# Moving the exponent multiplication of 64-bit weights from ScalarE to POOL

## The chip, the cores and the metric

The kernel runs on one core of a Trainium2 chip. A core has five engines that take instructions from queues of their own and wait for each other by semaphores: TensorE (PE, with its weight loads PEld), VectorE (DVE), ScalarE (ACT), GpSimd (POOL) and SyncE (SP), which here issues all transfers. The metric is the device time of one execution in microseconds (us).

## The reference

Four batches, eight heads, 768 positions, 64 dimensions a head. Attention is banded: a position sees the 127 before it, itself, and the first four ("sinks"). The attention's output is the input of a gated two-layer network.

```python
scores = q @ k.T / sqrt(64)
keep = (key < n_sink) | ((0 <= rel) & (rel < window))     # n_sink 4, window 128
a = softmax(where(keep, scores, -1e9));  x = a @ v        # x: (4, 768, 512)
h = maximum(x @ w_in, 0)                                  # w_in: 512 x 1024
conv = sum(conv_w[k] * shifted(h, k - 1) for k in 0..2)   # along the positions
out = (h * sigmoid(conv)) @ w_out                         # w_out: 1024 x 512
```

q, k and v are 32-bit floats. The three weights w_in, conv_w and w_out arrive as 64-bit floats.

## The kernel before

The work has three parts that run interleaved. Attention goes over pairs of heads: `scores` (lines 488 to 522) makes TensorE multiply, VectorE add the mask and find the smallest value (line 514), ScalarE take the exponential (line 517), VectorE sum and invert (519, 520), and POOL scale the result (line 522). `transp` then turns the tiles on TensorE (line 538 or 552), ScalarE copies them out (540 or 554), and `pv` multiplies by v. The network goes over units of 128 hidden features by 256 positions (`unit`, line 162): twelve multiplications into `ph` (line 183), the gate on ScalarE and VectorE (190 to 198), POOL's high and low part of the gated product (lines 200 and 201), and six multiplications into `po` (line 210). The main loop of `banded` (line 644) lays pieces of the network between the steps of attention.

The third part prepares the weights. `weights` (line 131) lists 17 pieces: eight of w_in (wi), eight of w_out (wo), each 128x512, and the taps of conv_w, 24x128. `need` (line 154) prepares them one by one, about one for each step of attention from the third on, and `fetch` (line 149) asks for the next transfers on SP's queue. A raw piece holds pairs of 32-bit words, and `narrow` (line 103) makes one 32-bit float of each pair: a multiplication of the high word, taken as a 32-bit float, by 2 to the power -112 (line 111), and three steps on VectorE which shift that by three bits and put in the top bits of the low word and the sign (lines 112 to 114). `split` (line 117) then has ScalarE write the rounded high part (line 121) and POOL the remainder (line 122).

The temporaries `w` and `low` of `narrow` come from three buffers (tag `st`, line 109), the raw pieces from three others (tag `nat`). A buffer is given out again when its last reader is done, so the multiplication of one piece can wait for the subtraction of an earlier one, and a load on SP for the second VectorE step of an earlier one.

The kernel is built with `schedule_with_timeline_sim=True` (line 821): a planner fixes the order of the instructions on each engine at build time, from the order of the program and from its own costs. On the chip each engine takes its instructions in that fixed order. All pieces of the trace here come from the branch `banded`.

Of the kernel before, what the change touches and what calls it, by code (L numbers as in the profile page):

```python
# [14 lines left out]
ALU = mybir.AluOpType  # L15
# [22 lines left out]
def f(ap):  # L38
    return ap.bitcast(F32)
# [21 lines left out]
class Moe:  # L61
# [41 lines left out]
    def narrow(self, raw):  # L103


        if raw.dtype == F32:
            return raw
        nc, (rows, n) = self.c.nc, raw.shape[0:2]
        w, low = (self.temp("st", 512, 3)[0:rows, 0:n] for i in range(2))
        lo, hi, wi, li = raw[:, :, 0], raw[:, :, 1], w.bitcast(I32), low.bitcast(I32)  # L110
        nc.scalar.mul(low, f(hi), 2.0 ** -112)
        nc.vector.tensor_scalar(wi, li, 3, None, ALU.logical_shift_left)
        nc.vector.scalar_tensor_tensor(out=wi, in0=lo, scalar=29, in1=wi, op0=ALU.logical_shift_right, op1=ALU.bitwise_or)  # L113
        nc.vector.scalar_tensor_tensor(out=wi, in0=li, scalar=-0x80000000, in1=wi, op0=ALU.bitwise_and, op1=ALU.bitwise_or)  # L114
        return w
# [709 lines left out]
```

## Time and profile before

| What | Value |
|---|---|
| Time, median of 3 runs | 495.17 us (494.23 to 495.84) |
| Span of the profiled execution | 492.3 us |
| The profiled execution's own time beside its span | not stated by the page; the runs' median is 2.9 us above the span |
| Instructions | 10616 |
| Busy: TensorE, ScalarE, VectorE, POOL | 460.4, 349.0, 341.1, 308.6 us |

The page's first part gives each engine's busy time and its share of the span. Its second part cuts the span into 40 equal slices of 12.3 us; each digit is the busy share of a slice in tenths, and PEclk is TensorE's granted clock in the same way. A line number such as L111 stands for line 111 of the kernel. In the tables by stretch each engine's busy time is followed by its number of instructions in brackets. In lists by time the columns are start, length, engine, line, operation, what is written from what, shape and count, and in square brackets the idle time before it with the instruction that ended it.

### The profile page before, as it was taken

What the parts mean: (1) busy time and instruction counts of PE and PEld (TensorE: products, weight loads), DVE (VectorE), ACT (ScalarE), POOL (GpSimd) and SP (SyncE); (2) the same over time, 40 slices, a digit from 0 to 9 for tenths busy, and PEclk for the clock granted to TensorE, in tenths of its full rate; (3) what the DMA queues carried; (4) which work ended last, traced back from release to release, by engine and by line L of the source; (5) the groups of instructions that cost most, each with busy time, mean ns of one, the idle gap of its engine ahead of it and who ended that gap; (6) DMA issues with size and microseconds to landing.
All of it is one profiled execution on the core that took longest, in us unless ns stands there. A gap on an engine that the chain in (4) does not pass through costs nothing.

```text
span 492.3 us, 10616 instructions
## 1 busy us (share of the span) xinstructions
PE 460.4 (94%) x3253; PEld 396.5 (81%) x3253; DVE 341.1 (69%) x1164; ACT 349.0 (71%) x1090; POOL 308.6 (63%) x582
## 2 busy tenths in 40 slices
PE   2878889899999999999999999999999999999994
PEld 1656678687887888888888888888889888999982
DVE  4678899847587787886677767776675664555551
ACT  3888897877797887886777777786776664535542
POOL 3467677845958787794867677684764554444341
PEclk9989899999999999999999999999999999999999
DMA  5877673427332423334042322224021100101001
GB/s 148 212 198 213 180 192 89 100 60 190 75 82 56 121 65 71 81 100 108 17 109 67 87 79 62 66 62 99 23 54 34 45 0 1 45 1 45 14 30 51
DMA packets 87306, 41.02 MB, mean 83 GB/s; under 512 B 80160, under 2 KB 80184, under 8 KB 87240
## 3 DMA queue, kind: packets, MB, share of 16 engines
q1 hardware_dynamic: 87240, 40.25, 31.3%
q8 instruction: 28, 0.46, 0.4%
q14 instruction: 38, 0.31, 0.2%
HBM read 27.60 MB, written 6.29 MB: 69 GB/s over the span
## 4 chain that ended last, share of the span: by engine, by line
PE 71%; DVE 7%; ACT 7%; POOL 6%; DMA 3%; issue 3%; SPq 1%; POOLq 0%; DVEq 0%; ACTq 0%
PE ph L183 25%; PE po L210 24%; PE px L591 6%; PE sc L337 3%; PE sc L338 3%; PE pts L552 3%; PE tq L271 2%; PE px L594 2%; ACT roomL L517 1%; PE tk L289 1%; DVE stm L114 1%; POOL pe L522 1%; DVE t L196 1%; DVE stm L113 1%; DMA wi_1r<-in_moe_w_in_dram 1%
## 5 line engine op out<-in xcount | busy, mean ns | idle before, releaser
L210 PE MATMUL po<-woH,g 128*128 128x512 f32 x384 | 141.6, 407 | 4.2 <-POOL g L200 4.2
L183 PE MATMUL ph<-xH,wiH 128*128 128x258 f32 (+1 forms) x384 | 113.2, 295 | 0.4 <-ACT xH L345 0.4
L183 PE MATMUL ph<-xL,wiH 128*128 128x258 f32 (+1 forms) x384 | 109.6, 286 | 0.0
L183 PE MATMUL ph<-xH,wiL 128*128 128x258 f32 (+1 forms) x384 | 109.5, 285 | 0.0
L200 POOL TENSOR_SCALAR g<-t 128x256 fp32r<-128x256 f32 x96 | 42.1, 439 | 63.6 <-DVE t L198 49.3
L210 PEld LDWEIGHTS po<-woH,g 128*128 128x128 f32 x384 | 68.8, 189 | 15.2 <-POOL g L200 5.5
L195 DVE SCALAR_TENSOR_TENSOR t<-hb,cw,t 128x256 f32<-128x256 f32 x96 | 55.1, 574 | 36.1 <-ACT t L194 35.4
L201 POOL TENSOR_TENSOR g<-t,g 128x256 fp32r<-128x256 f32 x96 | 75.9, 790 | 6.3
L522 POOL TENSOR_SCALAR pe<-pe,sm 128x132 f32<-128x132 f32 (+1 forms) x144 | 59.5, 425 | 30.7 <-DVE sm L520 20.6
L183 PEld LDWEIGHTS ph<-xH,wiH 128*128 128x128 f32 x384 | 73.1, 190 | 5.7 <-issue 1.6
L210 PE MATMUL po<-woL,g 128*128 128x512 f32 x192 | 75.8, 395 | 0.0
L183 PEld LDWEIGHTS ph<-xH,wiL 128*128 128x128 f32 x384 | 73.1, 190 | 2.2
L183 PEld LDWEIGHTS ph<-xL,wiH 128*128 128x128 f32 x384 | 72.9, 190 | 1.0 <-DVE xL L346 0.2
L517 ACT ACTIVATE pe<-pe,sm 128x132 f32<-128x132 f32 (+1 forms) x144 | 58.0, 405 | 14.1 <-DVE sm L514 13.5
L197 ACT ACTIVATE t<-t 128x256 f32<-128x256 f32 x96 | 40.3, 420 | 31.2 <-DVE t L196 30.5
L198 DVE SCALAR_TENSOR_TENSOR t<-t,hb 128x256 f32<-128x256 f32 x96 | 47.4, 494 | 17.7 <-ACT t L197 17.0
L196 DVE SCALAR_TENSOR_TENSOR t<-hb,cw,t 128x256 f32<-128x256 f32 x96 | 54.8, 570 | 4.4
L190 ACT ACTIVATE hb<-ph 128x258 f32<-128x258 f32 (+1 forms) x96 | 37.0, 386 | 29.2 <-PE ph L183 28.7
L194 ACT ACTIVATE t<-hb,cw 128x256 f32<-128x256 f32 x96 | 49.2, 513 | 7.1 <-POOL g L201 3.2
L556 POOL TENSOR_SCALAR_AFFINE_SELECT pT<-pT 128x256 f32<-128x256 f32 x60 | 29.4, 490 | 30.0 <-ACT pT L554 29.5
L513 DVE COPY_PREDICATED sc<-before,sc 128x128 f32<-128x128 int32 x120 | 34.0, 291 | 18.0 <-PE sc L338 17.1
L514 DVE CUSTOM_DVE_ANT_0 pe<-sc,m 128x132 f32<-128x132 f32 (+1 forms) x144 | 40.1, 289 | 7.7 <-PE sc L338 6.2
(148 smaller groups left out, 1005.9 us busy)
## 6 DMA issues: line engine op xcount, KB each, us to landing
raw<-in_q_dram SPq DMA_DIRECT2D x64, 96.0 KB
raw<-in_k_dram SPq DMA_DIRECT2D x64, 96.0 KB
out_dram<-stm SPq DMA_DIRECT2D x24, 256.0 KB
kk<-kk SPq DMA_DIRECT2D x24, 198.0 KB
vraw<-in_v_dram SPq DMA_DIRECT2D x24, 192.0 KB
wi_0r<-in_moe_w_in_dram SPq DMA_DIRECT2D x2, 512.0 KB
wi_1r<-in_moe_w_in_dram SPq DMA_DIRECT2D x2, 512.0 KB
wi_2r<-in_moe_w_in_dram SPq DMA_DIRECT2D x2, 512.0 KB
```

Of the source, the lines that this page charges most:

```text
L183: nc.tensor.matmul(u.h[:, 0:W], w[:, cc, ff * P:(ff + 1) * P], x[:, cc, t0:t1], start=(i == 0), stop=(i == len(prods) - 1))
L194: nc.scalar.mul(a, prev, cw[:, 0, ff:ff + 1])
L195: nc.vector.scalar_tensor_tensor(out=e, in0=this, scalar=cw[:, 1, ff:ff + 1], in1=a, op0=ALU.mult, op1=ALU.add)
L196: nc.vector.scalar_tensor_tensor(out=a, in0=nxt, scalar=cw[:, 2, ff:ff + 1], in1=e, op0=ALU.mult, op1=ALU.add)
L197: nc.scalar.activation(e, a, AF.Tanh)
L198: nc.vector.scalar_tensor_tensor(out=a, in0=e, scalar=1.0, in1=this, op0=ALU.add, op1=ALU.mult)
L200: nc.gpsimd.tensor_scalar(u.g[:, 0], a, 1.0, 1.0, ALU.mult, ALU.mult)
L201: nc.gpsimd.tensor_tensor(out=u.g[:, 1], in0=a, in1=f(u.g[:, 0]), op=ALU.subtract)
L210: nc.tensor.matmul(po[:, 0:c.DM], u.g[:, a, tt * P:(tt + 1) * P], w[:, ff, :], start=(ff == 0 and i == 0), stop=(ff == NFF - 1 and i == 2))
L514: nc.vector.tensor_tensor_reduce(out=pe[:, j, cols], in0=pc[:, P - at:SW][:, cols], in1=mk, op0=ALU.add, op1=ALU.min, scale=1.0, scalar=3. ...
L517: nc.scalar.activation(pe[:, j, cols], pe[:, j, cols], AF.Exp, bias=sm[:, j:j + 1], scale=-1.0, accum_out=sm[:, 2 + 2 * j:3 + 2 * j])
L522: nc.gpsimd.tensor_scalar(pe[:, j, cols], pe[:, j, cols], sm[:, 8 + j:9 + j], 1.0, ALU.mult, ALU.mult)
```

## The change

One line of `narrow` is replaced. The same product is computed by POOL; the second multiplication, by 1.0, leaves it as it is. The 17 instructions read every second 32-bit word of the raw piece and write a contiguous tile, as before.

```diff
55.00:62.00 7.00, 1.36 (x2) 0.81 0.56 149
62.00:70.00 8.00, 0.70 (x1) 1.00 0.70 200
70.00:75.00 5.00, 0.69 (x1) 1.00 0.67 187
75.00:90.00 15.00, 1.38 (x2) 1.00 0.28 63
 -108,7 +108,7 55.00:62.00 7.00, 1.36 (x2) 0.81 0.56 149
62.00:70.00 8.00, 0.70 (x1) 1.00 0.70 200
70.00:75.00 5.00, 0.69 (x1) 1.00 0.67 187
75.00:90.00 15.00, 1.38 (x2) 1.00 0.28 63

         nc, (rows, n) = self.c.nc, raw.shape[0:2]
         w, low = (self.temp("st", 512, 3)[0:rows, 0:n] for i in range(2))
         lo, hi, wi, li = raw[:, :, 0], raw[:, :, 1], w.bitcast(I32), low.bitcast(I32)
-        nc.scalar.mul(low, f(hi), 2.0 ** -112)
+        nc.gpsimd.tensor_scalar(low, f(hi), 2.0 ** -112, 1.0, ALU.mult, ALU.mult)
         nc.vector.tensor_scalar(wi, li, 3, None, ALU.logical_shift_left)
         nc.vector.scalar_tensor_tensor(out=wi, in0=lo, scalar=29, in1=wi, op0=ALU.logical_shift_right, op1=ALU.bitwise_or)
         nc.vector.scalar_tensor_tensor(out=wi, in0=li, scalar=-0x80000000, in1=wi, op0=ALU.bitwise_and, op1=ALU.bitwise_or)
```

## Rows read from the trace of the kernel before

**Rows 1.** The page's first part: busy time and share of each engine.

```profile
PE 460.4 (94%) x3253; PEld 396.5 (81%) x3253; DVE 341.1 (69%) x1164; ACT 349.0 (71%) x1090; POOL 308.6 (63%) x582
```

**Rows 2.** The table by stretch, four stretches of the span in us; after the length come PE, PEld, DVE, ACT and POOL busy, the granted clock, the share of the transfer engines and GB/s.

```profile
10.00:55.00 45.00, 35.16 (x212) 26.35 (x213) 34.66 (x123) 39.18 (x120) 25.25 (x37) 0.95 0.76 212
55.00:90.00 35.00, 32.55 (x247) 28.54 (x246) 31.85 (x78) 30.47 (x82) 27.41 (x30) 0.96 0.49 129
90.00:100.00 10.00, 7.88 (x41) 5.41 (x40) 8.25 (x31) 8.18 (x27) 8.28 (x14) 1.00 0.48 112
100.00:492.00 392.00, 383.34 (x2753) 335.02 (x2751) 262.17 (x918) 268.97 (x858) 243.63 (x479) 1.00 0.25 63
```

**Rows 3.** The same table for the instructions of line 111 alone; the second number is ScalarE's busy time.

```profile
10.00:55.00 45.00, 7.09 (x11) 0.95 0.76 212
55.00:62.00 7.00, 1.36 (x2) 0.81 0.56 149
62.00:70.00 8.00, 0.70 (x1) 1.00 0.70 200
70.00:75.00 5.00, 0.69 (x1) 1.00 0.67 187
75.00:90.00 15.00, 1.38 (x2) 1.00 0.28 63
```

**Rows 4.** What TensorE waited for, from 0 to 60 us and, the last row, from 60 to 130 us: total, times, longest.

```profile
PE trq L313 <- DMA raw<-in_q_dram: 3.2, 2, 2.9
PE sc L334 <- DVE sm L514: 3.1, 4, 1.5
PE tk L545 <- ACT sk L544: 1.9, 1, 1.9
...
PE po L210 <- POOL g L200: 3.0, 2, 2.0
```

**Rows 5.** The pieces of line 111 on the chain of work that ended last: start, length, what.

```profile
18.14 0.68 ACT stm L111
...
35.25 0.56 ACT stm L111
...
37.28 0.57 ACT stm L111
...
46.51 0.71 ACT stm L111
...
50.08 0.59 ACT stm L111
...
79.01 0.61 ACT stm L111
```

**Rows 6.** The table by stretch again (columns as in rows 2), for three stretches.

```profile
35.00:40.00 5.00, 4.91 (x40) 3.41 (x39) 4.79 (x24) 5.00 (x20) 2.53 (x5) 1.00 0.45 134
55.00:70.00 15.00, 15.00 (x123) 13.12 (x121) 13.84 (x42) 13.70 (x39) 11.01 (x14) 0.91 0.63 176
75.00:80.00 5.00, 4.60 (x41) 3.87 (x41) 4.88 (x9) 3.74 (x9) 2.55 (x2) 1.00 0.18 41
```

**Rows 7.** Waits around the multiplication: one instruction of POOL and one of ScalarE in order of time with the idle time before them, VectorE's wait for the multiplication between 10 and 90 us, and SP's wait before weight loads.

```profile
21.64 0.94 POOL L522 TENSOR_SCALAR roomH<-roomH,sm 128x260 f32<-128x260 f32 x2 [3.10 <-DVE sm L519]
...
46.51 0.71 ACT L111 ACTIVATE stm<-wo3r 128x512 f32<-128x512 f32 x1 [0.91 <-POOL woL L122]
...
DVE stm L112 <- ACT stm L111: 2.2, 3, 1.5
...
SPq L100 <- DVE stm L113: 16.4, 9, 3.3
```

**Rows 8.** POOL's nearest operations: two rows of a line's summary (shortest, median and longest in ns, first and last start) and two pairs in order of time.

```profile
L200 POOL TENSOR_SCALAR g<-t x96: 397/404/842, 71.2 to 484.0; 128x256 fp32r<-128x256 f32 x96
...
L122 POOL TENSOR_TENSOR wiL<-stm,wiH x8: 1262/1280/1718, 14.0 to 69.8; 128x512 fp32r<-128x512 f32 x8
...
22.55 0.72 POOL L522 TENSOR_SCALAR roomL<-roomL,sm 128x128 f32<-128x128 f32 x2
23.78 0.94 POOL L522 TENSOR_SCALAR roomL<-roomL,sm 128x260 f32<-128x260 f32 x2 [0.51 <-ACT wiH L121]
```

**Rows 9.** POOL, VectorE and TensorE in order of time around 70 us, POOL's next gap, and the third VectorE step of an earlier piece.

```profile
66.60 3.21 POOL L522 TENSOR_SCALAR roomL<-roomL,sm 128x260 f32<-128x260 f32 x4 [1.01 <-DVE sm L520]
69.78 1.43 POOL L122 TENSOR_TENSOR wiL<-stm,wiH 128x512 fp32r<-128x512 f32 x1
70.01 1.75 DVE L114 SCALAR_TENSOR_TENSOR stm<-stm,stm 128x512 int32<-128x512 int32 x1
72.07 0.50 PE L210 MATMUL po<-woH,g 128*128 128x512 f32 x1 [2.05 <-POOL g L200]
...
80.19 0.57 POOL L200 TENSOR_SCALAR g<-t 128x256 fp32r<-128x256 f32 x1 [2.39 <-DVE t L198]
...
38.72 0.68 DVE L114 SCALAR_TENSOR_TENSOR stm<-stm,stm 128x512 int32<-128x512 int32 x1
```

**Rows 10.** POOL and VectorE side by side: two scalings and the second VectorE step beside them, and the third VectorE step between 10 and 90 us as a group (busy us, mean ns).

```profile
29.92 1.37 POOL L522 TENSOR_SCALAR roomH<-roomH,sm 128x128 f32<-128x128 f32 x2 [1.19 <-DVE sm L520]
30.31 0.74 DVE L113 SCALAR_TENSOR_TENSOR stm<-wi_3r,stm 128x512 int32<-128x512 int32 x1
...
L114 DVE SCALAR_TENSOR_TENSOR stm<-stm,stm 128x512 int32<-128x512 int32 x16 | 16.5, 1029 | 0.1
```

## The prediction

> **What bounds the kernel now.** I read the page's busy shares first. TensorE is busy for 460.4 of 492.3 us, the next engine for 349.0 [rows 1], so the kernel is TensorE's over most of its length, and a change on other engines can only pay where TensorE stands idle. The table by stretch says where that is [rows 2]. From 100 us on TensorE is busy for 383.34 of 392.00 us. Between 10 and 55 us it is busy for 35.16 of 45.00, so idle for 9.8; between 55 and 90 us for 32.55 of 35.00, idle for 2.5; between 90 and 100 us idle for 2.1. All 17 instructions of the change lie between 10 and 90 us, eleven in the first of these stretches (7.09 us) and six in the second: two before 62 us, one in front of 70, one in front of 75 and two behind it, 4.13 us in all [rows 3]. What the change can win is therefore a part of about 12 us of idle time, and what it can lose is new idle time in the same place: every microsecond that the first 90 us get shorter or longer moves the TensorE-bound rest by as much.
>
> Next I read what TensorE waited for there [rows 4]. The input transfers' 3.2 us are not touched. Left are waits on VectorE's masked copies of the scores (3.1 us), on ScalarE (the longest 1.9 us) and, after 60 us, on POOL's high part of the gated product (3.0 us in two waits). So in this stage three engines take turns as the one that is late, and two of them have little room: between 10 and 55 us ScalarE is busy for 39.18 us of 45 (87%), VectorE for 34.66, POOL for 25.25; between 55 and 90 us VectorE leads with 31.85 of 35 (91%), ScalarE has 30.47, POOL 27.41 [rows 2].
>
> **What goes.** ScalarE loses 7.09 + 4.13 = 11.2 us, by the rows of the line itself. It falls to 32.1 of 45 us (71%) and 26.3 of 35 us (75%). Six of the 17 stand on the chain of waits, with 0.68, 0.56, 0.57, 0.71, 0.59 and 0.61 us, 3.7 us in all [rows 5]; that is the bound of what taking them off the chain gives, since the other eleven had something later beside them. I go through the six. The one at 18.14 us lies in a stretch where ScalarE's work follows without a gap until TensorE has waited 1.9 us for it, while POOL sat idle for 3.1 us [rows 7]: I count 0.6 gained. Those at 35.25 and 37.28 lie where TensorE is busy for 4.91 of 5.00 us [rows 6]; the cover there is TensorE's own work, and I count them at nothing (1.1 if that cover is gone). At 46.51 ScalarE stood 0.91 us waiting for the buffer that POOL's subtraction held before it could begin [rows 7]; on POOL that wait is gone, since the reader that holds the buffer is the instruction before it on the same queue. But the score copies that ScalarE does next come from VectorE, which was itself in a long third step of the unpacking, so of the 1.6 us (0.91 and 0.71) I count 0.6. At 50.08 VectorE waited for the result, and it will wait for POOL's in the same way: 0.2. The one at 79.01 lies where TensorE is 92% busy: nothing. The sum is -1.4 us, between 0 and -3.7 by the chain; with the 0.91 us wait in front of one of them, -4.6.
>
> **What comes.** POOL gets 16 operations of 128x512 and one of 24x128. The trace has no POOL operation with one input and 512 columns, and none that reads every second word, as this one does. The nearest row is the same form on 256 columns, 404 ns in the median and never under 397 [rows 8]. Two pairs of the softmax scaling give the price of a column: two of 260 columns take 0.94 us and two of 128 take 0.72, so 0.11 us for 132 columns, 0.83 ns each; 256 more columns make 404 + 213 = 617 ns. From below the bound is the 0.40 us of half the size; from above it is the two-input subtraction on 512 columns, 1.28 us in the median. I take 0.65 us, near the extrapolated row. That is 16 x 0.65 + 0.3 = 10.7 us (6.7 to 20.8): in the first stretch 6.8 us and in the second 3.9 us, which brings POOL to 32.1 of 45 (71%) and 31.3 of 35 (89%).
>
> Where this lies beside other work it is free, and in the first stretch it mostly does. Between 66.6 and 72 us it isn't: POOL runs four scalings, a weight subtraction and the first high part of a gated product without a gap, and TensorE stands 2.05 us for the last of them [rows 9]. The one multiplication between 62 and 70 us can fall in front of it: +0.65. Of those behind 75 us one or both fall into 2.39 us in which POOL waited for VectorE [rows 9], and the two between 55 and 62 lie where TensorE is never idle (15.00 of 15.00) [rows 6]; if either cover went, they would cost 0.65 each.
>
> Then VectorE. Its third unpacking step takes 0.68 us where nothing disturbs it, but 1.75 us beside a subtraction of POOL that had begun 0.2 us earlier and lasted 1.43 [rows 9]. It can also be POOL that pays: two scalings of 128 columns that take 0.72 us elsewhere took 1.37 beside the second step, which itself lost nearly nothing (0.74) [rows 10]. So the engines hold one another up, and a new POOL operation can hold VectorE up by as long as it lasts, or by nothing. I take half of an operation, 0.3 us, for the two multiplications between 62 and 75 us, where VectorE is 91% busy and TensorE isn't always full, and count one of the two as landing on a free VectorE: +0.3. The bounds are 0 and 6 x 0.65 = 3.9 for the whole second stretch.
>
> The Trainium skill, SBUF — State Buffer on-chip working memory, Summary: rules for kernel authors, says that VectorE and GpSimd don't share bandwidth there but exclude each other for whole instructions, when VectorE runs in a two-port mode or has two SBUF inputs and GpSimd reads SBUF. By that rule every multiplication that meets a second or third unpacking step, which read two tiles, holds it up to its own end or is held up itself; that is the case which rival 2 prices from rows. The trace agrees so far as its two cases in rows 9 and 10 go: in each, one engine lost about the remainder of the other's instruction.
>
> **What waits anew.** VectorE's shift by three waits for the multiplication; behind it on VectorE are score copies, and TensorE waits for those. Today that wait costs VectorE 2.2 us in three times [rows 7]. SP's queue is behind it too: a weight load waits until the second unpacking step has read an earlier buffer (16.4 us, nine times) [rows 7], and the q, k and v loads are queued behind it. If POOL is later than ScalarE, these are later; as POOL has 20 us without work in the first stretch, I cost it at nothing, and 2.2 us more if it is as late again as ScalarE was. Everything after 90 us is unchanged in kind.
>
> **Sum.** -1.4 + 0.65 + 0.3 = -0.45 us. It is made against the profiled execution, whose span is 492.3 us; the page gives no other time for it, and the median of the runs, 495.17, lies 2.9 us above that span, so I take the difference over to the median: 494.7 us. By its bounds: -4.6 + 0 at the best end, and 0 + 3.9 + 0.65 at the worst, less the covers.
>
> **Rivals.** (1) The relief of ScalarE counts in full: at 87% busy it is the most loaded engine of the first stretch, and a shorter queue there brings every exponential and every copy forward, also those beside which the chain now runs. For it speak the ScalarE waits in rows 4 and POOL's idle time; against it VectorE, at 77% and 91%, which doesn't lose work. It would give -3.7 on the chain and +0.65: 492.1 us. (2) Slower: POOL and VectorE become the bound from 55 us on. Place: the six multiplications after 55 us, in POOL's and VectorE's fullest stretch; price: 0.65 us each, 3.9 us, against at most 0.9 us that the first stretch has won by then; it decides as soon as POOL finds less than about 4 us idle in these 35 us, that is if an operation takes 1.28 us rather than 0.65 (27.41 + 7.7 = 35.1 of 35). That gives +3.0: 498.2 us. For it speak [rows 9, 10], against it the full TensorE between 55 and 70 us [rows 6]. (3) The move does what it says but the order matters more: the program's order on each engine is written by a planner at build time, and a changed cost there can bring other instructions forward. Nothing in the trace gives this a sign; within 2 us of today by the size of TensorE's single longest waits [rows 4], either way.
>
> **How the numbers follow.** The forecast gets 0.42, its own range 492.9 to 496.6. Rival 1 gets 0.28, rival 2 0.25, rival 3 0.05. A measurement of this kernel can tell about 0.3% from no change, 1.5 us. Of the forecast's chance 0.07 lies below 493.7, 0.03 above 496.7; rival 1 gives 0.26 of faster, rival 2 0.25 of slower, rival 3 splits. Together: faster 0.35, same 0.34, slower 0.31. The range from 490.8 to 499.0 takes in most of both rivals.
>
> **What would show it.** In the changed profile line 111 must stand on POOL, 17 times, about 0.62 to 0.75 us each; over 1.0 us would speak for rival 2. ScalarE's busy time must be lower by about 11 us between 10 and 90 us. The idle time of TensorE between 10 and 55 us should fall from 9.8 to about 8.5 us, that between 55 and 100 us should rise from 4.6 to about 5.5. If VectorE's third unpacking step, in the mean 1.03 us, grows to 1.3 or more, the price of the mutual hold-up was set too low. The forecast is wrong if TensorE's idle time before 100 us changes by more than 2 us in sum, or if that after 100 us changes by over 1 us, which no step here accounts for.

## The result and the profile after

The changed kernel takes 501.07 us in the median (499.56 to 501.66, four runs), beside 495.21 us (494.23 to 495.84, four runs) for the kernel before: ratio 1.0116, 95% interval 1.0095 to 1.0138. It is slower, by 5.7 us on 495.2, and lies outside the range of 490.8 to 499.0 us. (In the code cut of the change further up, four lines of [rows 3] stand twice ahead of the code; they are figures of the profile. The change is the one line with the minus and the one with the plus.)

One reading aid first. The changed kernel's profiled execution took 499.56 us with a span of 497.8, and in the runs below an execution's own time is likewise 1.7 to 1.9 us above its span. For the profile of before, whose own time wasn't stated, the span of 492.3 us so means about 494.1 us, the quick end of its runs. Two profiles can therefore stand some 2 us further apart, or closer, than two medians. Differences in us below are the ratio to before taken on 495.2 us, unless a trace is named.

Busy shares of the changed kernel, which answer to [rows 1]:

```profile
PE 462.9 (93%) x3253; PEld 395.3 (79%) x3253; DVE 349.6 (70%) x1164; ACT 340.6 (68%) x1073; POOL 321.2 (65%) x599
```

Its table by stretch, the columns as in [rows 2], and then the same table for the instructions of line 111 alone, which answers to [rows 3]:

```profile
10.00:55.00 45.00, 34.27 (x223) 25.53 (x224) 36.00 (x121) 34.49 (x111) 32.29 (x47) 1.00 0.76 205
55.00:90.00 35.00, 29.12 (x207) 24.01 (x206) 33.48 (x77) 24.08 (x65) 31.22 (x35) 0.90 0.47 131
90.00:100.00 10.00, 9.46 (x56) 7.89 (x54) 6.70 (x21) 7.73 (x24) 8.73 (x13) 1.00 0.35 76
...
10.00:95.00 85.00, 12.06 (x17) 0.96 0.62 168
```

The move did what it says: between 10 and 90 us ScalarE is busy for 58.6 us instead of 69.7, and POOL makes the 17 multiplications in 12.06 us, 0.71 in the mean (0.74 for the 16 of 128x512). But TensorE's idle time rose in both long stretches, from 9.84 to 10.73 us (45.00 less 34.27) and from 2.45 to 5.88; only between 90 and 100 us did it fall, from 2.12 to 0.54. In sum it is 17.2 us instead of 14.4. VectorE, which lost and gained no instruction, is busy for longer: 36.00 against 34.66 and 33.48 against 31.85 [rows 2].

The three unpacking steps of VectorE show where. The table for 10 to 95 us, for lines 112, 113 and 114 alone; before first:

```profile
10.00:95.00 85.00, 8.99 (x17) 0.96 0.63 171
10.00:95.00 85.00, 12.39 (x17) 0.96 0.63 171
10.00:95.00 85.00, 16.73 (x17) 0.96 0.63 171
```

And after:

```profile
10.00:95.00 85.00, 12.60 (x17) 0.96 0.62 168
10.00:95.00 85.00, 14.77 (x17) 0.96 0.62 168
10.00:95.00 85.00, 14.55 (x17) 0.96 0.62 168
```

The same 17 pieces, the same instructions, and 41.9 us instead of 38.1. The first step, with a single input, grew by 40%. That the third fell isn't the move's doing: with ScalarE multiplying in the changed kernel's order (e2 below) it takes 13.98 us, and the three together 35.8, so that in its own order the move lengthened them by 6.1 us. One piece of the timeline after shows how (start, length, engine, line):

```profile
33.22 0.29 POOL L111 TENSOR_SCALAR stm<-tapsr 24x128 f32<-24x128 f32 x1
33.50 0.93 POOL L522 TENSOR_SCALAR roomH<-roomH,sm 128x260 f32<-128x260 f32 x2
33.55 2.19 DVE L112 TENSOR_SCALAR stm<-stm 24x128 int32<-24x128 int32 x1 [0.80 <-POOL stm L111]
34.40 1.25 POOL L122 TENSOR_TENSOR wiL<-stm,wiH 128x512 fp32r<-128x512 f32 x1
...
36.42 0.24 PE L128 MATMUL cwt<-ident,stm 24*128 24x24 f32 x1 [2.68 <-DVE stm L114]
```

VectorE is released by POOL's multiplication, but POOL, in order, goes straight on to two scalings and a subtraction. The small step begins 0.05 us after the scalings and ends at 35.74, just after the subtraction does at 35.65: 2.19 us for 24x128. TensorE waits 2.68 us for the result. That wait is new beside those in [rows 4].

### The profile page after: what moved, and what is told of

Its sections match the earlier page's. It is cut to its first block, busy times and chain, and to the rows that moved or that the text cites. A ratio compares the mean times of both kernels' runs of the same rounds, so it can differ in the third digit from the quotient of the medians.

```text
span 497.8 us, 10601 instructions
## 1 busy us (share of the span) xinstructions
PE 462.9 (93%) x3253; PEld 395.3 (79%) x3253; DVE 349.6 (70%) x1164; ACT 340.6 (68%) x1073; POOL 321.2 (65%) x599
## 4 chain that ended last, share of the span: by engine, by line
PE 75%; DVE 8%; POOL 4%; ACT 3%; issue 2%; DMA 1%; SPq 0%; POOLq 0%; ACTq 0%; DVEq 0%
PE ph L183 25%; PE po L210 25%; PE px L591 7%; PE sc L337 3%; PE pts L552 3%; PE sc L338 3%; PE tq L271 2%; PE px L594 2%; DVE stm L113 1%; DVE stm L114 1%; PE tk L289 1%; PE px L583 1%; DVE stm L112 1%; DVE t L196 1%; POOL roomH L522 1%
## 5 line engine op out<-in xcount | busy, mean ns | idle before, releaser
L195 DVE SCALAR_TENSOR_TENSOR t<-hb,cw,t 128x256 f32<-128x256 f32 x96 | 55.7, 581 | 34.6 <-ACT t L194 33.7
L196 DVE SCALAR_TENSOR_TENSOR t<-hb,cw,t 128x256 f32<-128x256 f32 x96 | 56.3, 587 | 4.2
L337 PE MATMUL sc<-kk,X 128*128 128x260 f32 (+1 forms) x144 | 42.4, 305 | 0.5 <-DVE sm L514 0.5
```

The costliest lines, as they stand in the source:

```text
L195: nc.vector.scalar_tensor_tensor(out=e, in0=this, scalar=cw[:, 1, ff:ff + 1], in1=a, op0=ALU.mult, op1=ALU.add)
L196: nc.vector.scalar_tensor_tensor(out=a, in0=nxt, scalar=cw[:, 2, ff:ff + 1], in1=e, op0=ALU.mult, op1=ALU.add)
L337: self.nc.tensor.matmul(pc, X[:, j, u, :], kk[:, j, lo:hi], start=True, stop=False)
```

## The experiments

In most kernels every engine is held, by dependences that order instructions without a semaphore, to the order that the planner wrote for the kernel before, or for the changed kernel ("order of after"). So the instruction itself and the planner's new order are told apart. In the traces TensorE's 3253 multiplications stand one for one in the order named in the table. Holding the order of before with nothing else changed wasn't run; e4, the nearest to it, costs 1.1 us at the most. All in one table; the three steps are VectorE's busy time in lines 112 to 114 between 10 and 95 us of the one profiled execution (38.1 before, 41.9 after). A difference between two rows is less certain than either interval.

| Run | What is different | Order | Ratio, 95% interval | us | Three steps |
|---|---|---|---|---|---|
| e1 | POOL multiplies | before | 1.0073 (1.0053 to 1.0093) | +3.6 | 42.0 |
| e2 | ScalarE multiplies | after | 1.0022 (1.0002 to 1.0042) | +1.1 | 35.8 |
| e3 | spare POOL multiplication | before | 1.0074 (1.0061 to 1.0087) | +3.7 | 40.9 |
| e4 | POOL multiplies one column | before | 1.0008 (0.9994 to 1.0022) | +0.4 | 40.7 |
| e5 | first nine on POOL | before | 1.0034 (1.0022 to 1.0046) | +1.7 | 40.7 |
| e6 | nobody multiplies | before | 0.9933 (0.9920 to 0.9947) | -3.3 | 40.3 |
| e7 | spare POOL memset | before | 1.0038 (1.0016 to 1.0060) | +1.9 | 41.1 |
| e8 | spare POOL multiplication | after | 1.0146 (1.0128 to 1.0163) | +7.2 | 39.8 |
| e9 | POOL multiplies one column | after | 1.0075 (1.0056 to 1.0093) | +3.7 | 39.0 |
| e10 | weights without multiplication | planner's own | 1.0007 (0.9995 to 1.0020) | +0.3 | 36.8 |
| e11 | weights without multiplication | before | 0.9956 (0.9940 to 0.9972) | -2.2 | 39.7 |
| e12 | spare VectorE op, 17 x 128x128 | before | 1.0028 (1.0015 to 1.0041) | +1.4 | 38.0 + 4.3 spare |
| e13 | 16 tiny POOL memsets a piece | before | 1.0054 (1.0040 to 1.0068) | +2.7 | 40.3 |
| e14 | spare VectorE op, 5 x 128x512 | before | 1.0056 (1.0041 to 1.0071) | +2.8 | 37.7 + 4.5 spare |
| e15 | the taps back on ScalarE | after | 1.0078 (1.0057 to 1.0099) | +3.9 | 40.3 |

**The move or the order: e1, e2.** e1 has the change's line of code, e2 the line of before; the order is added behind the kernel's building (`hold`, which sets the dependences, isn't shown):

```diff
-            banded(c)
+            banded(c); hold(c)
```

> The multiplication on POOL, but every engine's instructions in the order that the planner wrote for the kernel before (the 17 multiplications stand on POOL at the place that the planner's list gave them). Theory A (the price of the move itself: VectorE's unpacking held up by POOL and waiting for it, 3.8 us of longer steps and 3.0 us of longer waits in the changed kernel): 499 to 502 us, about as slow as the changed kernel. Theory B (the new order that the planner wrote costs it, the move itself little, as forecast): 494 to 497 us.

> The multiplication on ScalarE as before, but every engine's instructions in the order that the planner wrote for the changed kernel. Theory A (price of the move): 494 to 497 us, as fast as before. Theory B (the order): 499 to 502 us with ScalarE's version too.

The move costs 3.6 us where nothing else changes (498.70 us, just below the first range of its expectation). The planner's new order costs 1.1 us by itself, 0.1 to 2.1 by the interval, and between the two ways of multiplying in that order lie 1.0116 - 1.0022, 4.7 us. So the price is in the main the move's, and in the new order the whole is 2.1 us dearer (1.0116 - 1.0073).

Since e1 has TensorE's instructions in the order of before, each can be compared by its start. It is 2.0 us early at 30.5 us (before 30.51), 0.6 late at 35, 2.2 late at 44, 3.8 at 63, 5.2 at 95, and 5.3 at the end of the kernel. The 2.0 us aren't all ScalarE's relief. Between 27 and 30 us the trace of before has TensorE at a granted clock of 0.50, its lower level of 1.2 GHz, and e1 has it at 1.00. So has e13 below, in which ScalarE multiplies as before, and it is 1.3 us early at the same place. The table (columns as in [rows 2]) for before, e1 and e13:

```profile
27.00:30.00 3.00, 3.00 (x24) 2.23 (x21) 2.42 (x8) 3.00 (x13) 0.35 (x3) 0.50 0.37 83
27.00:30.00 3.00, 3.00 (x33) 2.71 (x32) 2.96 (x6) 1.59 (x8) 1.35 (x4) 1.00 0.61 135
27.00:30.00 3.00, 3.00 (x29) 2.44 (x29) 2.30 (x6) 3.00 (x13) 1.49 (x19) 1.00 0.62 135
```

About 0.7 us is left for the relief in e1, and it is gone 5 us later. What TensorE waits for in e1 in the first 60 us, against 3.1 us in four times before [rows 4]:

```profile
PE sc L334 <- DVE sm L514: 5.4, 6, 2.3
```

e2 and the changed kernel have one order too. Against e2 the changed kernel is 1.6 us early at 33 us (the clock is 1.00 in both, so that here the relief shows by itself), 0.4 late at 35, behind the taps, 1.5 late at 60, 3.1 at 63 and 4.7 at 99. Between 60 and 63 TensorE again waits for VectorE:

```profile
60.69 0.71 PE L334 MATMUL sc<-kks,X 128*128 128x260 f32 x2 [1.58 <-DVE sm L514]
```

**Late, relieved or merely present: e3, e4, e6.**

```diff
         nc.scalar.mul(low, f(hi), 2.0 ** -112)
+        nc.gpsimd.tensor_scalar(self.spare[0:rows, 0:n], f(hi), 2.0 ** -112, 1.0, ALU.mult, ALU.mult)
```

> All engines keep the order of the kernel before. ScalarE still makes the 17 multiplications for VectorE; behind each, POOL makes the same multiplication once more, into a spare tile that nobody reads, at the place that it has in e1. So POOL is as occupied as in e1, and nobody waits for its result. Theory 'occupied' (the instruction itself costs: it runs beside VectorE's unpack steps and stands in front of POOL's own work): +4 us as in e1, or up to +6 since ScalarE gets no relief here, 498.5 to 500.5 us. Theory 'late' (what costs is that VectorE's first step waits until POOL comes to the multiplication): nothing, 494.3 to 495.3 us.

```diff
-        nc.scalar.mul(low, f(hi), 2.0 ** -112)
+        nc.scalar.mul(low[:, 1:n], f(hi)[:, 1:n], 2.0 ** -112)
+        nc.gpsimd.tensor_scalar(low[:, 0:1], f(hi)[:, 0:1], 2.0 ** -112, 1.0, ALU.mult, ALU.mult)
```

> All engines keep the order of the kernel before. POOL multiplies 1 of the columns of each piece and ScalarE the others, so VectorE's first step waits for both, and POOL is occupied for some 0.1 us a piece rather than 0.78. Theory 'late': most of the +4 us of e1 without its relief of ScalarE, 497.5 to 500.5 us. Theory 'occupied': at most a fifth of it, 494.5 to 495.5 us.

```diff
-        nc.scalar.mul(low, f(hi), 2.0 ** -112)
-        nc.vector.tensor_scalar(wi, li, 3, None, ALU.logical_shift_left)
+        nc.vector.tensor_scalar(wi, hi, 3, 0x3FFFFFFF, ALU.logical_shift_left, ALU.bitwise_and)
...
```

The third step then takes the sign from `hi` instead of `li`.

> All engines keep the order of the kernel before. Nobody multiplies: VectorE's first step takes the raw high words, shifts them by 3 and clears the top exponent bit in the same instruction, which for weights below 2 in magnitude gives the same bits. So this is ScalarE's relief alone, with VectorE's wait gone too. Theory that the relief reaches the end (TensorE stood 1.8 us earlier at 28 to 30 us in e1): 491.0 to 493.4 us. Rival that another engine, VectorE above all, takes its place by 35 us: 494.0 to 495.3 us.

e3 decides between late and present: an instruction for which no engine waits for data costs 3.7 us, as much as the move. e4, with the wait and less work, costs 0.4, within its interval nothing. (Its POOL instruction still takes 0.32 us in the mean, more than the 0.1 that was expected.) And e6 shows what might have been won had nobody taken the work over: 3.3 us. It leaves the multiplication out for the taps too, which go beyond 2 in magnitude, so it is no version to use, and it takes away more than ScalarE's work: VectorE's wait for the product and one of the two temporaries of a piece. The three prices don't add up to the move's: 3.7 + 0.4 - 3.3 is 0.8 us, measured are 3.6. Why so little of the relief is collected beside the hold-ups stays open.

**Where: e5.**

```diff
-        nc.scalar.mul(low, f(hi), 2.0 ** -112)
+        nc.gpsimd.tensor_scalar(low, f(hi), 2.0 ** -112, 1.0, ALU.mult, ALU.mult) if self.done < 9 else nc.scalar.mul(low, f(hi), 2.0 ** -112)
```

> All engines keep the order of the kernel before. POOL makes the first 9 multiplications (the first half's wi pieces, the taps, wo0 to wo3), ScalarE the last 8. In e1 TensorE's instructions stood 2.9 us late at 44 us, after the first nine, and 5.5 us at 74 us, after all. If each stretch keeps its own loss, +2.2 to +3, 496.8 to 497.7 us. If the last eight alone make the end late (what is lost early is got back in the second stretch's idle time), 494.0 to 495.3 us.

The median of 497.42 us lies in the first range; by the ratio the first nine cost 1.7 of the 3.6 us, about half. Neither stretch has the loss to itself.

**What of the presence costs: e7, e12, e13, e14.**

```diff
         nc.scalar.mul(low, f(hi), 2.0 ** -112)
+        nc.gpsimd.memset(self.spare[0:rows, 0:n + n * 3 // 16], 0.0)
```

> As e3 (order of the kernel before, ScalarE multiplies for VectorE), but the spare POOL instruction is a memset of 128x608, which reads nothing; by the kernel's own memsets of 128x792 (0.84 us) and 128x128 (0.20 us) it holds POOL for about 0.66 us, as long as e3's multiplication undisturbed. Theory 'shared reading' (VectorE is held up while POOL streams operands from SBUF, and that is the price): VectorE's three steps take about 38 us as in the kernel before, and the time is 494.3 to 496.0 us. Theory 'POOL's queue' (POOL's own splits and gates come 0.7 us later each, and that is the price): 498 to 499.5 us, with VectorE's steps near 38 us. If the time is 498 or more and VectorE's steps take 41 us or more, a memset holds VectorE up like a multiplication.

Neither came out: +1.9 us. Lines 113, 114 and 115 of e7, which are the three steps:

```profile
10.00:95.00 85.00, 11.97 (x17) 0.94 0.63 169
10.00:95.00 85.00, 12.37 (x17) 0.94 0.63 169
10.00:95.00 85.00, 16.76 (x17) 0.94 0.63 169
```

A memset reads nothing, and lengthens the first step by 3.0 us (8.99 to 11.97) and the second and third by nothing. e3's multiplication, which reads, has 10.60, 13.78 and 16.52: it lengthens the first and the second. The two don't hold POOL equally long, though: e7's memsets take 9.7 us in all, e3's multiplications 13.9, and a part of e7's lower price may be that.

```diff
         nc.vector.tensor_scalar(wi, li, 3, None, ALU.logical_shift_left)
+        nc.vector.tensor_scalar(self.spare[0:rows, 0:128], f(hi)[:, 0:128], 2.0, 1.0, ALU.mult, ALU.mult)
```

> Order of the kernel before, ScalarE multiplies, POOL has nothing new. Behind the first unpacking step of each piece VectorE makes one spare multiplication of 128x128 (some 0.22 us by its other instructions of that size), 17 times, 3.5 to 3.8 us in all: as much longer as VectorE was in e3 (3.2) and e1 (4.7). Theory that VectorE's longer steps alone are the price: 2.5 to 4 us more than before, 497.5 to 499.2 us. Rival that VectorE has room and the price lies in POOL's own work coming later: at most 1 us more, 494.3 to 496 us.

```diff
         nc.scalar.mul(low, f(hi), 2.0 ** -112)
+        for i in range(16):
+            nc.gpsimd.memset(self.spare[0:rows, i:i + 1], 0.0)
```

> As e3 (order of the kernel before, ScalarE multiplies for VectorE), but in place of the spare multiplication POOL makes 16 memsets of 128x1 for each piece. By the kernel's own memsets of that size, which start some 0.04 us apart, they hold POOL for 0.6 to 0.7 us, as the multiplication does, but none of them is long enough to hold VectorE up by more than about 0.1 us. Theory that POOL's own work coming later makes up what e12 leaves of e3's price (+3.9 less about 1.4): 2 to 3 us more than before, 497.1 to 498.3 us. Rival that POOL has room, and that the rest lies in VectorE's hold-ups being long and falling in the wrong places: at most 0.8 us more, 494.3 to 496.0 us.

```diff
+        if self.done in (4, 7, 8, 9, 15):
+            nc.vector.scalar_tensor_tensor(out=self.spare, in0=self.spare, scalar=1.0, in1=self.spare, op0=ALU.mult, op1=ALU.mult)
         nc.vector.tensor_scalar(wi, li, 3, None, ALU.logical_shift_left)
```

> Order of the kernel before, POOL has nothing new. VectorE makes one spare two-source multiplication of 128x512 (0.7 us or a little less by the kernel's own two-source steps) in front of the first unpacking step of five pieces, the taps, wo2, wo3, the first wi piece of the second half and wo6, the pieces in which e3 held VectorE up longest: 3.4 us in sum, less than e12's 4.6 spread over 17 pieces. Theory that long hold-ups in the wrong places are dearer than the same time spread out: 2 to 3.5 us more than before, 497.1 to 498.7 us. Rival that VectorE's time alone counts and place does not: 0.7 to 1.3 us more, 495.8 to 496.6 us.

The spare VectorE work lasted 4.3 us in e12 and 4.5 in e14, but cost 1.4 us spread over 17 pieces (neither expectation) and 2.8 in five lumps (its first one): five long hold-ups in the places where e3 held VectorE up longest are about twice as dear as the same time spread out. The two also differ in form: e14's operation has two inputs and stands in front of the first step, e12's has one and stands behind it. Whether e14's 2.8 us is less than e3's 3.7 isn't shown, as the intervals overlap. e13 was meant to have POOL occupied without holding VectorE up, and didn't quite: its three steps take 40.3 us, 2.2 more than before, although no memset in it is wider than one column. Its 2.7 us therefore hold both causes. What stays open is how e3's price divides between VectorE's hold-ups and POOL's own work coming later; that both are in it is likely, and not separated here.

**The changed kernel's own order: e8, e9, e15.** e8 and e9 have the edits of e3 and e4. e15 has POOL multiply where `rows == P` and ScalarE otherwise, so for the taps alone.

> As e3, but every engine keeps the order of the changed kernel: ScalarE multiplies for VectorE, POOL makes the same multiplication once more into a spare tile at the changed kernel's place. With ScalarE alone this order took 494.88 us (e2), the changed kernel takes 501.07. If the instruction's presence beside VectorE is the price here too: +4 to +6 on e2, 498.9 to 501 us. If in this order the wait for POOL's place in its queue is what adds the last 2 us over e1: 498.5 to 499.3 us, and e9 shows the missing 2. If it is the wait alone: 494.5 to 495.5 us.

> As e4, in the order of the changed kernel: POOL multiplies 1 column of each piece, ScalarE the others, and VectorE waits for both. If the wait for POOL's place in its queue costs about 2 us in this order: 496.5 to 498 us. If it costs nothing, as in e4: 494.5 to 495.6 us.

> As the changed kernel, in its own order, but the one multiplication of the taps (24x128) is ScalarE's again; the 16 of 128x512 stay on POOL. In the changed kernel VectorE's first step on the taps lasted 2.19 us beside two POOL instructions in a row, against 0.24 us in the same order with ScalarE multiplying (e2), and TensorE waited 2.7 us for the taps. Theory that this one hold-up is a part of its own, about the 2 us by which the changed kernel is slower than e1: 1.3 to 2.3 us less than the changed kernel's 501.1, 498.7 to 499.8 us. Rival that the loss is taken back or taken elsewhere, since all the other multiplications are still on POOL: 500.4 to 501.6 us.

Against e2, which has the same order, presence costs 6.1 us (1.0146 - 1.0022) and the one column 2.6, where in the order of before they cost 3.7 and 0.4. The same instruction has another price in each order. Both times lie above the ranges expected for those causes (502.42 and 498.91 us), and that e9's 2.6 us are the price of waiting isn't shown. VectorE's waits for the product between 10 and 100 us are, in e2, in e9 (two rows) and in the changed kernel:

```profile
DVE stm L112 <- ACT stm L111: 4.8, 5, 1.9
...
DVE stm L112 <- ACT stm L111: 2.9, 2, 1.9
DVE stm L112 <- POOL stm L111: 1.4, 2, 0.7
...
DVE stm L112 <- POOL stm L111: 5.2, 5, 1.8
```

e9 waits no longer than e2; what is longer in it is the three steps, 39.0 us against 35.8. e8 shows the dearest single place, the taps again; line 113 is the first step there:

```profile
35.13 0.29 POOL L112 TENSOR_SCALAR spare<-tapsr 24x128 f32<-24x128 f32 x1
35.14 3.10 DVE L113 TENSOR_SCALAR stm<-stm 24x128 int32<-24x128 int32 x1 [0.45 <-POOL roomL L505]
35.41 0.93 POOL L523 TENSOR_SCALAR roomH<-roomH,sm 128x260 f32<-128x260 f32 x2
36.31 1.25 POOL L123 TENSOR_TENSOR wiL<-stm,wiH 128x512 fp32r<-128x512 f32 x1
37.54 0.63 POOL L112 TENSOR_SCALAR spare<-wo0r 128x512 f32<-128x512 f32 x1
```

The same step in e2, without the spare instruction in front:

```profile
34.81 1.00 POOL L522 TENSOR_SCALAR roomH<-roomH,sm 128x260 f32<-128x260 f32 x2
34.82 0.24 DVE L112 TENSOR_SCALAR stm<-stm 24x128 int32<-24x128 int32 x1 [0.44 <-POOL roomL L504]
```

In e2 it starts within 0.01 us of the scalings and takes 0.24 us. In e8 the spare multiplication of 0.29 us starts first, and the step ends at 38.24, after five POOL instructions (the scalings are two). e15 takes only this event out of the changed kernel:

```profile
32.12 0.23 DVE L112 TENSOR_SCALAR stm<-stm 24x128 int32<-24x128 int32 x1 [0.49 <-POOL roomL L504]
...
33.30 0.24 PE L128 MATMUL cwt<-ident,stm 24*128 24x24 f32 x1 [0.69 <-DVE stm L114]
```

The step is back at 0.23 us, TensorE has the taps at 33.30 instead of 36.42, and the kernel takes 498.94 us: 1.9 us less (1.0116 - 1.0078), 0.4 to 3.4 by the two intervals. One instruction of 24x128 so makes about a third of the change's loss. The two profiled executions don't differ in time (499.54 and 499.56 us): at 99 us e15 is 2.3 us ahead of the changed kernel, and between 120 and 129 us it loses 2.1 of that, waiting at first and then at the lower clock:

```profile
124.00:128.00 4.00, 4.00 (x24) 3.31 (x21) 1.30 (x6) 1.14 (x6) 3.43 (x8) 0.57 0.32 87
```


**A faster version: e10, e11.** The weights w_in and w_out go without a multiplication as in e6, which is right below 2 in magnitude; for the taps ScalarE multiplies as before.

> The planner is free to choose its order again. For the 16 weight pieces VectorE's first step takes the raw high words, shifts by 3 and clears the top exponent bit, which is right for weights below 2 in magnitude; the taps are multiplied by ScalarE as before. e6 gave 491.93 with no multiplication at all in the order of before. If the relief stands in a free order too: 490.5 to 493.0 us. If the planner's order gives it back: 494 to 496 us.

> As e10 (16 weight pieces without a multiplication, the taps multiplied by ScalarE), but all engines keep the order of the kernel before. If e10's loss of e6's gain came from the planner's new order: as e6, 491.0 to 493.0 us. If it came from the taps' multiplication: 494 to 496 us.

e11 takes 493.38 us (492.22 to 493.81) against 495.19 for the kernel before beside it: 0.4% faster (0.3 to 0.6), and faster than the changed kernel too. It holds only for w_in and w_out below 2 in magnitude. With the planner free the gain is gone (e10). So the work is worth removing, but the order that the planner then writes has to be looked at as well.

## Where the microseconds sit: fewer of them in idle time than it seems

With the order held, TensorE does the same 482 matmuls before its 483rd starts, six of them before 10 us. The table from 10 us to that start splits each run's delay into TensorE's busy and idle time. Before:

```profile
10.00:95.55 85.55, 72.14 (x476) 57.66 (x477) 71.62 (x216) 74.02 (x215) 58.08 (x74) 0.96 0.63 171
```

e1, and below it two of its stretches of 5 us:

```profile
10.00:100.73 90.73, 76.24 (x476) 60.63 (x477) 76.23 (x217) 66.82 (x199) 71.12 (x92) 0.91 0.60 162
...
30.00:35.00 5.00, 1.19 (x7) 0.70 (x5) 4.16 (x11) 3.09 (x8) 4.65 (x6) 0.98 0.81 247
35.00:40.00 5.00, 4.72 (x15) 3.42 (x16) 3.87 (x19) 3.25 (x12) 3.23 (x6) 0.50 0.32 107
```

e3:

```profile
10.00:100.49 90.49, 75.40 (x476) 60.38 (x477) 74.78 (x217) 75.08 (x217) 72.57 (x92) 0.92 0.60 163
```

e6:

```profile
10.00:93.97 83.97, 68.72 (x476) 54.52 (x477) 74.04 (x216) 65.71 (x199) 59.46 (x74) 1.00 0.66 176
```

e1 reaches the 483rd matmul 5.2 us later than before. Only 1.1 us of that is more idle time (90.73 - 76.24 = 14.5 against 13.4); 4.1 us is the same matmuls taking longer, at a mean granted clock of 0.91 instead of 0.96. In e3 it is 1.7 and 3.3. In e6 idle time even grew by 1.8 us, and the gain is wholly in busy time, at a clock of 1.00. The two stretches show it close up: between 30 and 35 us TensorE works 1.19 us of 5, and in the next 5 us the clock is at 0.50, its lower level of 1.2 GHz. The same score multiplications, before and in e1 (where a fifth joins them without a gap):

```profile
36.49 1.04 PE L334 MATMUL sc<-kks,X 128*128 128x260 f32 x4
38.19 2.41 PE L334 MATMUL sc<-kks,X 128*128 128x260 f32 x5
```

That is 0.26 and 0.48 us each. The Trainium skill, TensorE: Matmul & The Clock Gate, HAM oscillation — how this bites in real kernels, describes this: waits between bursts throttle the clock, and the next burst starts slow; the trace agrees here. These are single executions, in which the clock also varies by itself (the trace of before has its own stretches at the lower level, one of them shown above), so the split is a reading of these profiles and not of the medians.

## Why the prediction was wrong

- **What bounds it: the place right, the currency not.** In e1 all is won and lost before 100 us; from there to the end its delay changes from 5.2 to 5.3 us. But "a change on other engines can only pay where TensorE stands idle" left TensorE's clock out of the sum, without a reason: of e1's 5.2 us only 1.1 lies in idle time, and e6's gain lies wholly in busy time. TensorE's idle time between 10 and 100 us rose by 2.7 us in the changed kernel, more than the 2 us that were named as a sign of being wrong.
- **ScalarE's relief, -1.4: too small, and not collected.** With nobody multiplying the gain was 3.3 us (e6) and 2.2 (e11), around rival 1's 3.1, though both runs take away more than ScalarE's work. In the move some 0.7 us of it shows at 30 us in e1, 1.6 at 33 us in the changed kernel against e2, and nothing by 35 us in either.
- **The duration of the operation, 0.65 us: nearly right.** The 16 of 128x512 took 0.74 in the mean. That POOL would stand in front of TensorE's wait near 70 us (+0.65) came out smaller: in e1 that wait takes 3.2 us in two times, before 3.0 [rows 4], and in the changed kernel's own order TensorE doesn't have it between 60 and 130 us.
- **VectorE held up, +0.3: this step failed.** The text counted one of two multiplications between 62 and 75 us, at half an operation, and bounded the rest by the second stretch. Measured in the sum of the three steps were 3.9 us in the order of before (e1), 3.0 of them in the first eleven pieces, which the text took to be covered, and 6.1 in the changed kernel's own order (against e2); and e3 shows 3.7 us of time for an instruction that is merely there, POOL's own work coming later included. The sentence that let it through is "where this lies beside other work it is free, and in the first stretch it mostly does": POOL's idle time there was cover for POOL, not for VectorE.
- **The wrong indicator.** The text named the third step as the one to watch. In the order of before its time stayed, 16.73 us and 16.59 in e1, in the changed kernel it fell with the order, and the first and second grew. The rule that I drew on was read too narrowly, as one on steps with two inputs. The Trainium skill, SBUF — State Buffer, Who interferes with whom, also names VectorE's one-input scalar form among those that can take the port pair which GpSimd uses, and says that a two-input form contends only with a GpSimd instruction that reads. Both agree with e7: beside a memset the first step grew by 3.0 us, the two-input steps by nothing. e13 agrees less well: beside memsets alone its first step grew by 1.3 us and its second by 0.8. The hint was in the trace of before too, where the taps' first step took 1.27 us for 24x128.
- **The new wait, at nothing, with 2.2 us if POOL is late.** VectorE waits 5.2 us for the product in the changed kernel, 3.0 more than before [rows 7], but 4.8 in the same order with ScalarE multiplying (e2), and 3.2 in e1: most of the longer wait is the order's. What it costs in time isn't separated; e4 and e9 have it together with a small POOL instruction, at 0.4 and 2.6 us. The value of nothing was chosen by POOL's idle time, which says nothing of whether POOL is free when VectorE asks.
- **The rivals.** Rival 2 had the sign, the engines and nearly the time of e1 (498.2, measured 498.7). That is in part luck: its condition, operations of 1.28 us, wasn't met, and half of the loss lies before its place. Rival 3 gave the order 2 us either way; the order's own part is 1.1 us (e2), and what it seems to add to the move's price is about as much again (4.7 in it, 3.6 in the order of before), though that difference isn't clear of the intervals.

## What to carry to other kernels

Moving an instruction to an engine with idle time isn't free if that engine holds up the one that is next to become the bound: price it by what it does to the neighbour, at every place, and watch the small instructions that release TensorE most. To find out what a move costs, hold the order of before and add the moved instruction as a spare one that nobody waits for. And remember that a longer wait of TensorE can be paid a second time in the matmuls behind it, when the clock falls as it did in e1.

## What the runs showed that was not expected

VectorE, once it has lost to a POOL instruction, need not get its turn when that one ends: the 24x128 step lasted through three POOL instructions in the changed kernel (2.19 us) and through five in e8 (3.10 us), each time to 0.1 us behind the last, and took 0.24 us where it began level with POOL (e2). It isn't always so. In e9 the step began 0.05 us behind the scalings too, and ended before them:

```profile
35.52 0.93 POOL L522 TENSOR_SCALAR roomH<-roomH,sm 128x260 f32<-128x260 f32 x2
35.57 0.49 DVE L112 TENSOR_SCALAR stm<-stm 24x128 int32<-24x128 int32 x1 [0.68 <-POOL stm L111]
```

What decides is open. Memsets of 128x1, 88 ns each in the median, came with 2.2 us more of VectorE's steps in sum (e13), where e12 and e14, with nothing new on POOL, stay within 0.4 us of before. And the sum of VectorE's steps doesn't rank the runs: e4 has 40.7 us, as e5 has, at 0.4 us instead of 1.7, so where a hold-up falls seems to count as well as how much there is.
